# Attention with a routed mixture of experts: an own order for each of a batch's four attention periods, fixed PSUM places, and one FP32 product for a block of scores

## Chip, cores and metric

The kernel runs on one core of a Trainium2 chip. The metric is the device time of one execution in microseconds (us); of several executions the median is taken.

## What is computed

Eight batches, each with 8 heads of 576 positions by 64 dimensions, go through attention with a mask that lets a block of 64 positions see itself and the blocks before it. The result is 4608 rows of 512 numbers. Each row chooses one of 4 groups and in it one of 4 experts, is sent through that expert's two matrices (512 by 1024 and 1024 by 512, ReLU between) and is scaled by the two softmax weights.

```python
scores = scale * np.matmul(q, k.transpose(0, 1, 3, 2))
mask = block_i >= block_j                       # blocks of 64 positions
attn = softmax(np.where(mask, scores, -1e9))
x = np.matmul(attn, v).transpose(0, 2, 1, 3).reshape(4608, 512)
g_idx = argmax(x @ w_group);  e_idx = argmax(x @ w_expert[g_idx])
out[t] = g_w[t] * e_w[t] * (relu(x[t] @ w1[g, e]) @ w2[g, e])
```

## The kernel before

The program has an attention stage and an expert stage. Attention works on **head pairs**: pair `i` is two heads of one batch, 32 pairs in all, four to a batch. All five engines are scheduled by hand: each engine runs its instructions in the order in which the program writes them, and a semaphore holds an instruction back until its inputs are there and its output place is free.

**Periods and tokens.** `period` (line 357) is called with `x` from 0 on. It walks through a list of tokens, `ORDER` (lines 52 to 58); a token such as `S2@0` or `T1@1` is a step and a lag, and is done for pair `x - lag`. So one period mixes steps of several pairs, and one list serves all periods. A letter behind the lag says which engine drains a PSUM tile or does a conversion: `d` is DVE, `a` is ACT (POOL for `h` and `l`). The steps of a pair, with the line that does them:

- `K` (`prep`, line 160): the tiles of k and q are transposed by PE into PSUM; `k0`, `k1` (`full`) copy them to `nf`, as FP32. The last 64 positions of k and q go through another PSUM tile, the one that `V` fills (`flip_last`), and `j0`, `j1` (`full_last`) copy them to `nf`.
- `h0`, `h1` (`high`, line 191) round `nf` to FP32R (an FP32 number of fewer bits) in `qk`, k first and then q; `l0`, `l1` (`low`, line 196) subtract the rounded part, so that `qk` holds a high and a low part of each number. In the list `h0`, `h1` and `l1` are on POOL, `l0` on DVE.
- `S1`, `S2`, `S3`, `S8` (`score`, line 204): PE makes the scores as three products, high by high, high by low and low by high (`PROD`). `S2` also makes the scores of the first block of 128 queries, with the same three products into the columns from 384 of its PSUM tile. Two small products add the mask.
- `D` (`rowmax`, line 236) takes each row's maximum on DVE; `E0` to `E8` (`expo`, line 241) take the exponentials on ACT, with the row sums.
- `T1` to `T4` (`trans`, line 254): PE transposes the exponentials into PSUM; `t0` to `t4` (`drain`) copy them to `pt`. `V` (`values`, line 290) multiplies by v into the tile `o`; `v` copies that to `xT`.
- The **router's** steps `R`, `X`, `L`, `n`, `Y`, `M`, `G`, `Z` (`token`, line 649) exist once in a batch, not once in a pair: the logits, the choice of an expert, the writing of rows (`xd`) and of table entries (`tab`, `Z`). With one list for all, the lag alone decides in which of the four periods of a batch each of them falls.

The PSUM tiles of attention come from one pool of four places of two banks, handed out in turn (`wide`, line 94): the fifth tile that is asked for waits for the readers of the first.

The last period runs the list `END`. Its hooks (`timed`, in `attention_moe`) issue the first gathers and scatters of the expert stage. That stage is a list of groups of matmuls on PE, with the weights' loads and their splitting into high and low parts planned alongside; its last row store is split between ACT and DVE (`store`, lines 1160 and 1161). A loop for rows that did not fit (`overflow`, line 1341) follows; its count, `cnti`, is written by DVE in `spill`, and every engine loads it.

Of the kernel before, what the change touches and what calls it, by code (L numbers as in the profile page):

```python
# [8 lines left out]
F32 = mybir.dt.float32  # L9
# [5 lines left out]
ALU = mybir.AluOpType  # L15
# [52 lines left out]
class Attention:  # L68
    def __init__(self, tc, ctx, inner, q, k, v, consts):
# [9 lines left out]
        self.ps2 = self.psx.enter_context(tc.tile_pool(name="ps2", bufs=4, space=PSUM))  # L79
# [9 lines left out]
        self.mk = pfix.tile([P, 2, BLK], BF16, name="mk")  # L89
        self.lds, self.rs, self.xTs, self.sms = {}, {}, {}, {}  # L90
# [113 lines left out]
    def score(self, i, u):  # L204
# [17 lines left out]
        for u, c0 in ((2, 0), (0, 384)) if u == 2 else ((u, 0),):  # L222
            w = P * (u + 1)
            st = r["s", u] = ps[:, :, c0:c0 + w]
            for x, (hq, hk) in enumerate(self.PROD):
                for z in range(2):
                    p = slice(64 * z, 64 * z + 64)
                    nc.tensor.matmul(st[:, z, :], lhsT=t[p, hq, S + P * u:S + P * u + P], rhs=t[p, hk, 0:w],  # L228
                                     start=x == 0 and c0 == 0, stop=False)
        m = 2 if u == 0 else 1  # L230
# [93 lines left out]
    def start(self, N, order, on_dve, init):  # L324
# [17 lines left out]
        self.on_dve = on_dve  # L342
# [27 lines left out]
    def token(self, i, tok, N):  # L370
# [54 lines left out]
class Router:  # L425
# [187 lines left out]
    def spill(self, at, row, cnti):  # L613
# [32 lines left out]
        V.tensor_copy(cnti[0:1, 0:1], g[0:1, 0, R - 1:R])  # L646
        yield

    def token(self, at, b, tok):
# [61 lines left out]
        elif k == "Z":  # L711
            self.scatter(b, st, j, at.gate(at.now, 3) if j == 3 and not at.closed else None)
# [130 lines left out]
class Moe:  # L843
# [302 lines left out]
    def store(self, s, c, full):  # L1146
# [12 lines left out]
        elif s.get("o") == len(self.slots) - 1:  # L1159
            nc.scalar.activation(ys[0:n, 0:256], y[0:n, 0:256], AF.Copy, scale=cw[0:n])  # L1160
# [201 lines left out]
def attention_moe(ctx, tc, q, k, v, w_group, w_expert, w1, w2, out, order=None, on_dve=None):  # L1362
# [16 lines left out]
    with tc.manual_schedule(engines={ET.PE, ET.Activation, ET.DVE, ET.Pool, ET.SP}):  # L1379
# [81 lines left out]
        for _ in run:  # L1461
            pass
# [27 lines left out]
```

## Time and profile before

| what | value |
|---|---|
| median of 3 executions | 788.81 us (788.7 to 791.23) |
| the profiled execution | 785.75 us |
| its span, first to last instruction | 784.0 us |
| mean granted TensorE clock over the span | 0.996 |
| PE, ACT, DVE, POOL busy in the span | 97%, 64%, 69%, 45% |

The profile is of one execution. Engines are PE (matrix products; PEld is its weight load), ACT, DVE, POOL and SP (which issues most of the DMAs). Shares over the span average two stages: attention up to about 335 us, experts from there on. Each row of the page gives a source line, an engine, an operation, and output and input by the program's names.

### The profile page before, as it was taken

Reading aid. Unit: us, or ns where it says so; the run is one execution under the profiler, and the core shown is the slowest. Engines: PE = TensorE matmul, PEld = TensorE weight load, DVE = VectorE, ACT = ScalarE, POOL = GpSimd, SP = SyncE. Lnnn points to the kernel's source line nnn. Section 1 sums busy time; section 2 is a strip of 40 time slices with the busy share of each in tenths; the row PEclk is TensorE's granted clock in tenths of the full one; section 3 lists DMA queues with packets and bytes.
Section 4 is the critical chain, followed back from the end, with each engine's and each line's share of the span. In section 5 each row is a group of like instructions: output and inputs, shape, how many; then the busy total and the mean of one; then the engine's idle time right before and its main releaser. Section 6 shows DMA issues by size and latency. Waiting matters only on the chain.

```text
span 784.0 us, 20180 instructions
## 1 busy us (share of the span) xinstructions
PE 759.1 (97%) x7422; PEld 620.5 (79%) x7422; DVE 544.7 (69%) x1153; ACT 500.4 (64%) x1244; POOL 350.2 (45%) x481
## 2 busy tenths in 40 slices
PE   7899999999999999999999999999999999999996
PEld 4677777777777787768888788788988888888874
DVE  5567888888888888885454654754666667777742
ACT  5999999999999998755433433432434545545622
POOL 6444345454545454344143644454551553544212
PEclk9999999999999999999999999999999999999999
DMA  6478464646464636443779979979778897787771
GB/s 137 96 210 237 116 137 109 139 109 139 108 139 108 140 102 159 166 123 117 271 203 225 365 228 237 287 223 219 245 200 234 267 268 188 204 250 231 261 245 42
DMA packets 219108, 146.71 MB, mean 187 GB/s; under 512 B 155558, under 2 KB 186870, under 8 KB 219008
## 3 DMA queue, kind: packets, MB, share of 16 engines
q1 hardware_dynamic: 209920, 120.76, 57.6%
q0 software_dynamic: 9088, 24.64, 9.9%
q8 instruction: 60, 0.98, 0.5%
q14 instruction: 40, 0.33, 0.1%
HBM read 113.46 MB, written 24.59 MB: 176 GB/s over the span
## 4 chain that ended last, share of the span: by engine, by line
PE 80%; ACT 7%; DVE 6%; issue 3%; POOL 2%; DMA 2%; POOLq 0%; SPq 0%; ACTq 0%; DVEq 0%
PE h L1050 18%; PE y L1114 18%; PE o L313 10%; PE s L228 7%; PE tp L157 6%; PE h L1043 4%; PE s L218 3%; ACT pb L251 3%; PE ye L1114 3%; ACT pt L284 3%; PE he L1050 3%; PE y L1122 2%; DVE wl L949 1%; PE y L1133 1%; PE lg L690 1%
## 5 line engine op out<-in xcount | busy, mean ns | idle before, releaser
L1050 PE MATMUL h<-xt,wh 128*128 128x264 f32 (+6 forms) x704 | 156.3, 312 | 2.4 <-DVE xt L1010 2.3
L251 ACT ACTIVATE pb<-s,nm 128x128 f32<-128x128 f32 (+4 forms) x288 | 156.1, 568 | 3.5 <-DVE nm L239 1.6
L949 DVE TENSOR_TENSOR wl<-raw,wh 128x512 fp32r<-128x512 f32 x192 | 147.3, 804 | 8.5 <-ACT wh L948 8.4
L239 DVE TENSOR_REDUCE nm<-s 128x2 f32<-128x768 f32 (+4 forms) x160 | 126.3, 806 | 34.1 <-PE s L234 29.9
L1050 PEld LDWEIGHTS h<-xt,wh 128*128 128x128 f32 x704 | 119.2, 188 | 18.2 <-issue 4.2
L948 ACT CAST wh<-raw 128x512 fp32r<-128x512 f32 x192 | 109.6, 618 | 8.6 <-DMA raw<-in_moe_w_dram 6.0
L284 ACT COPY pt<-tp 128x1024 f32<-128x1024 f32 (+4 forms) x160 | 105.3, 696 | 8.6 <-PE tp L157 6.4
L1050 PE MATMUL h<-xt,wl 128*128 128x264 f32 (+6 forms) x352 | 109.2, 310 | 0.0
L1114 PE MATMUL y<-wh,hring 128*128 128x512 f32 x306 | 106.9, 400 | 0.4 <-ACT ys L1165 0.2
L228 PE MATMUL s<-qk 64*128 64x384 f32 (+3 forms) x768 | 89.9, 343 | 6.4 <-POOL qk L199 3.0
L1167 POOL DMA_INDIRECT out_dram<-ys,ids x40 | 47.0, 1174 | 108.1 <-DVE ys L1163 88.3
L313 PE MATMUL o<-pt,vb 128*64 128x320 f32 (+4 forms) x896 | 93.6, 360 | 0.4 <-DVE tmp L708 0.2
L194 POOL CAST qk<-nf 128x640 fp32r<-128x640 f32 (+1 forms) x63 | 42.7, 701 | 98.1 <-DVE nf L281 71.4
L313 PEld LDWEIGHTS o<-pt,vb 128*64 128x64 f32 x896 | 59.3, 137 | 32.2 <-DVE tmp L708 0.3
L157 PE MATMUL tp<-ident,pb 64*128 64x64 f32 x1600 | 76.3, 226 | 1.6 <-DVE xT L281 1.1
L228 PEld LDWEIGHTS s<-qk 64*128 64x128 f32 x768 | 61.6, 188 | 15.0 <-POOL qk L199 6.1
L157 PEld LDWEIGHTS tp<-ident,pb 64*128 64x128 f32 x1600 | 63.8, 140 | 10.2 <-ACT pb L251 3.9
L982 POOL COPY pl<-xg 128x1024 int16<-128x1024 int16 (+3 forms) x35 | 40.3, 1154 | 62.3 <-DMA xg<-xd,ids 40.6
L1114 PEld LDWEIGHTS y<-wh,hring 128*128 128x128 f32 x306 | 57.4, 188 | 13.1 <-DVE hring L1061 0.5
L1050 PEld LDWEIGHTS h<-xt,wl 128*128 128x128 f32 x352 | 66.2, 188 | 1.2
L251 ACT ACTIVATION_READ_ACCUMULATOR pb<-s,nm 128x1 f32 x288 | 64.1, 223 | 0.0
L199 POOL TENSOR_TENSOR qk<-nf,qk 128x640 fp32r<-128x640 f32 x31 | 61.2, 1975 | 2.6
(255 smaller groups left out, 1324.0 us busy)
## 6 DMA issues: line engine op xcount, KB each, us to landing
raw<-in_moe_w_dram SPq DMA_DIRECT2D x96, 512.0 KB, 4.2
rawq<-in_moe_w_dram SPq DMA_DIRECT2D x24, 512.0 KB, 7.8
natk<-in_k_dram SPq DMA_DIRECT2D x32, 256.0 KB, 3.6
natq<-in_q_dram SPq DMA_DIRECT2D x32, 256.0 KB, 5.5
vb<-in_v_dram SPq DMA_DIRECT2D x64, 128.0 KB, 2.8
wh<-in_moe_w_dram SPq DMA_DIRECT2D x16, 512.0 KB, 5.0
xd<-xns SPq DMA_DIRECT2D x12, 512.0 KB, 3.2
tab<-fill POOLq DMA_DIRECT2D x10, 512.0 KB, 4.1
```

The costliest lines, as they stand in the source:

```text
L157: self.nc.tensor.transpose(out=out[:, z], in_=src[r], identity=self.c["ident"][r, r])
L199: (eng or self.side(("l", n))).tensor_tensor(out=r["qk"][:, 1, o], in0=r["nf"][:, o], in1=r["qk"][:, 0, o].bitcast(F32), op=ALU.subtract)
L228: nc.tensor.matmul(st[:, z, :], lhsT=t[p, hq, S + P * u:S + P * u + P], rhs=t[p, hk, 0:w], start=x == 0 and c0 == 0, stop=False)
L239: self.nc.vector.tensor_reduce(out=o, in_=r["s", u], op=ALU.max, axis=ax, negate=True)
L251: nc.scalar.activation(reg, src, AF.Exp, bias=r["nm"][:, t:t + 1], accum_out=self.sms[b][:, pr, z, u:u + 1])
L284: return self.nc.scalar.copy(dst, src)
L313: nc.tensor.matmul(o[64 * a:64 * a + 64, hf, c0:c0 + BLK * (b1 - t)], lhsT=r["v"][:, a, j, :], rhs=pt[:, PTJ * j + t:PTJ * j + b1, a, :], ...
L948: nc.scalar.copy(h[:, sl], s["raw", u][:, sl])
L949: nc.vector.tensor_tensor(out=l[:, sl], in0=s["raw", u][:, sl], in1=h[:, sl].bitcast(F32), op=ALU.subtract)
L1050: nc.tensor.matmul(o, lhsT=ww[:, dc, f], rhs=rr[:, dc, t], start=dc == 0 and x == 0, stop=dc == 3 and x == 2)
L1114: nc.tensor.matmul(y[c][0:n], lhsT=hh, rhs=w, start=k == 0 and x == 0, stop=k == 7 and x == 2)
L1167: i = nc.gpsimd.indirect_dma_start(out=self.out, out_offset=bass.IndirectOffsetOnAxis(ap=s["ids"][0:n, c, 0:1], axis=0), in_=ys[0:n], in_o ...
```

## The change

1. `ORDER` becomes five lists. Period `x` runs list `x % 4`, and the first four periods run the fifth list. So each of a batch's four periods has its own order and its own choice of engines (`on_dve` is set anew in each period). `END` is another list as well.
2. The PSUM pool has one buffer for each of four tags, and a string of digits says for each tile, in the order in which tiles are asked for, which of the four places it takes.
3. `h` and `l` are cut differently: the first 512 columns of k and of q are rounded together in one instruction as soon as `k0` and `k1` are there, the last 64 of k and the last 128 of q apart from them (`kt`, `qt`); the low parts are four instructions, in three tokens.
4. The first block of scores, in `S2`, is one FP32 product of `nf` in place of the three FP32R products.
5. Every scatter `Z` is held back by the last row maximum written before it; `cnti` is copied by POOL, after the run; the last row store is ACT's alone; the hooks of the last periods sit at other places.

```diff
-ORDER, ON_DVE = parse("""
-Z2@7 E3@1 S2@0 D2@0 Z4@8 E2@1 n1@3a E8@1 T1@1 t3@1a t1@1a D0@0 K@-1 Z0@10 Y1@4 S3@0 D3@0 G2@6 R0@3
...
+ORDERS = [parse(t) for t in """
+t3@1a S2@0 E8@1 K@-1 S3@0 E2@1 V@2 E3@1 k1@-1a G0@5 k0@-1a D2@0 h0@-1a T2@1 D0@0 D3@0 S8@0 T1@1 Z4@9 E1@0 E4@0
+T4@1 E0@0 E5@0 E7@0 E6@0 G1@5 j1@-1d j0@-1d t0@1a v@2d h1@-1a l1@-1a l0@-1a S1@0 T3@0 l2@-1a D8@0 t2@1a t4@1d
+D1@0 t1@1a
+|
...
+""".split("|")]
...
+SLOTS = """
+3210123013201230213210312031231021302132130231023021031023103210231201302103231013202130231023021023021302310213
...
-        self.ps2 = self.psx.enter_context(tc.tile_pool(name="ps2", bufs=4, space=PSUM))
+        self.ps2 = self.psx.enter_context(tc.tile_pool(name="ps2", bufs=1, space=PSUM))
...
-        return self.ps2.tile([P, 2, 512], F32, tag="W", name=name)
+        return self.ps2.tile([P, 2, 512], F32, tag=f"W{next(self.slots)}", name=name)
...
+    def part(self, t, n):
+
+        if n == "kq":
+            return t[:, 0:2 * S].rearrange("p (n c) -> p n c", c=S)[:, :, 0:512]
+        return t[:, dict(k=slice(0, 512), q=slice(S, S + 512), kt=slice(512, S), qt=slice(S + 512, 2 * S + BLK))[n]]
...
-        (eng or self.side(("h", n))).tensor_copy(r["qk"][:, 0, o], r["nf"][:, o])
+        eng.tensor_copy(self.part(r["qk"][:, 0], n), self.part(r["nf"], n))
...
-        for u, c0 in ((2, 0), (0, 384)) if u == 2 else ((u, 0),):
-            w = P * (u + 1)
...
+        if m == 2:
+            st = r["s", 0] = ps[:, :, 384:512]
+            for z in range(2):
+                p = slice(64 * z, 64 * z + 64)
+                nc.tensor.matmul(st[:, z, :], lhsT=r["nf"][p, S:S + P], rhs=r["nf"][p, 0:P], start=True, stop=False)
...
+        self.last_gate = o[0:1, 0:1]
...
-        self.high(0, 0, nc.vector)
-        self.high(0, 1)
-        self.low(0, 0, nc.vector)
-        self.low(0, 1, nc.vector)
+        self.high(0, "k", nc.vector)
+        self.high(0, "q", nc.gpsimd)
+        self.low(0, "k", nc.vector)
+        self.low(0, "q", nc.vector)
+        for n in ("kt", "qt"):
+            self.high(0, n, nc.gpsimd)
+        for n in ("kt", "qt"):
+            self.low(0, n, nc.gpsimd)
...
-            self.high(i, tok[1])
+            for n in ("kt", "qt") if tok[1] else ("kq",):
+                self.high(i, n, self.side(tok))
         elif k == "l":
-            self.low(i, tok[1])
+            for n in (("k",), ("q",), ("kt", "qt"))[tok[1]]:
+                self.low(i, n, self.side(tok))
...
-        V.tensor_copy(cnti[0:1, 0:1], g[0:1, 0, R - 1:R])
+        self.over = g[0:1, 0, R - 1:R]
...
-            self.scatter(b, st, j, at.gate(at.now, 3) if j == 3 and not at.closed else None)
+            self.scatter(b, st, j, None if at.closed else at.last_gate)
...
-            nc.scalar.activation(ys[0:n, 0:256], y[0:n, 0:256], AF.Copy, scale=cw[0:n])
-            nc.vector.tensor_scalar(out=ys[0:n, 256:512], in0=y[0:n, 256:512], scalar1=cw[0:n], scalar2=None, op0=ALU.mult)
+            nc.scalar.activation(ys[0:n], y[0:n], AF.Copy, scale=cw[0:n])
...
+            order, at.on_dve = ORDERS[x % 4 if x > 3 else 4]
...
             for _ in run:
             pass
+        nc.gpsimd.tensor_copy(cnti, ro.over)
```

What the new lists do to the engines is seen in the instructions that each engine gets. In a row, `L` is the line, then the operation, and the tile it writes and those it reads. The first place is POOL in one steady period (the third batch's, one pair). Before:

```order
L812 MEMSET mark 1x1
L819 DMA tab<-pay_163,pi_2026 82560x16
L779 IOTA pay_164 128x5
L194 CAST qk_113<-nf_115 128x576
L194 CAST qk_113<-nf_115 128x640
L199 TENSOR_TENSOR qk_113<-nf_115,qk_113 128x640
```

and with the change:

```order
L851 COPY mark<-nm_2470 1x1
L856 DMA tab<-pay_163,pi_2032 82560x16
L221 CAST qk_114<-nf_116 128x64
L221 CAST qk_114<-nf_116 128x128
L225 TENSOR_TENSOR qk_114<-nf_116,qk_114 128x512 x2
L225 TENSOR_TENSOR qk_114<-nf_116,qk_114 128x64
L225 TENSOR_TENSOR qk_114<-nf_116,qk_114 128x128
L221 CAST qk_113<-nf_115 128x2x512
```

Both low parts of the 512 columns are now POOL's, the rounding of the next pair (`128x2x512`) stands ahead of everything that needs the last columns, and the scatter's hold copies from `nm`, the row maxima, where a MEMSET stood.

The second place is PE at the step `S2`, in the same batch. Before:

```order
L157 MATMUL tp_3_2470<-ident,pb_120 128x64 x16
L228 MATMUL s_2_2499<-qk_113 128x384 x6
L228 MATMUL s_2_2499<-qk_113 128x128 x6
L234 LDWEIGHTS mq
L234 MATMUL s_2_2499<-mk,mq 128x2x64
```

and with the change:

```order
L253 MATMUL s_2_2471<-nf_115 128x128 x2
L259 MATMUL s_2_2471<-qk_113 128x384 x6
L265 LDWEIGHTS mq
L265 MATMUL s_2_2471<-mk,mq 128x2x64
```

Two products of `nf` stand ahead of the six of `qk`, in place of six behind them.

The third place is ACT over most of one period. Before:

```order
L251 ACTIVATE pb_119,sm_2496<-s_3_2546,nm_2498 128x512 x2
L284 COPY pt_2469<-tp_2_2581 128x2x3x128
L738 ACTIVATE eex_2629<-edd_2625 128x20
L284 COPY pt_2469<-tp_2_2581 128x256
L284 COPY pt_2469<-tp_4_2609 128x2x5x64
L251 ACTIVATE pb_119,sm_2496<-s_1_2598,nm_2498 128x256 x2
L251 ACTIVATE pb_119,sm_2496<-s_8_2636,nm_2498 128x576
L284 COPY pt_2676<-tp_3_2677 128x2x4x128
L284 COPY pt_2676<-tp_1_2722 128x2x2x128
L284 COPY nf_115<-tp_2734 128x512
L285 ACTIVATE nf_115<-tp_2734 128x512
```

and with the change, in the period whose list has both logit copies (`lt`):

```order
L316 COPY lt<-lg_1_2850 128x2x288
L316 COPY lt<-lg_0_2859 128x2x288
L316 COPY pt_2893<-tp_3_2894 128x2x4x128
L283 ACTIVATE pb_120,sm_2468<-s_1_2881,nm_2685 128x256 x2
L283 ACTIVATE pb_119,sm_2468<-s_3_2921,nm_2920 128x512 x2
L316 COPY nf_116<-tp_2947 128x512
L283 ACTIVATE pb_119,sm_2468<-s_2_2932,nm_2920 128x384 x2
L283 ACTIVATE pb_119,sm_2468<-s_2_2932,nm_2920 128x128 x2
L316 COPY pt_2893<-tp_1_2998 128x2x2x128
L316 COPY pt_2893<-tp_2_3010 128x256
L316 COPY pt_2893<-tp_2_3010 128x2x3x128
```

One of the two copies to `nf` and the copy of `tp_4` are gone from ACT in this period. Over the whole program ACT has 13 scaled and 10 plain copies to `nf` fewer, 7, 3 and 17 copies to `pt` fewer (of 256, 768 and 640 columns), and 11 copies to `xT` (576 columns) more; DVE has the reverse, and 23 subtractions fewer. On PE, between two `V` steps of a steady batch, 15 instructions wait for PE itself before, and 7 with the change.

## Rows read from the trace of the kernel before

**Rows 1.** Page, part 1: busy time, share of the span, instructions

```profile
PE 759.1 (97%) x7422; PEld 620.5 (79%) x7422; DVE 544.7 (69%) x1153; ACT 500.4 (64%) x1244; POOL 350.2 (45%) x481
```

**Rows 2.** Windows by stage: start:end length, busy (instructions), granted PE clock, DMA share, GB/s

```profile
19.20:28.80 9.60, 7.87 (x113) 6.66 (x111) 5.85 (x9) 9.37 (x27) 4.33 (x5) 0.82 0.48 96
...
106.74:117.08 10.34, 10.20 (x172) 7.92 (x171) 8.60 (x16) 10.05 (x28) 4.75 (x7) 1.00 0.78 173
...
126.44:135.76 9.32, 9.32 (x152) 7.49 (x153) 8.03 (x17) 9.18 (x27) 4.49 (x6) 1.00 0.61 150
...
185.18:224.43 39.25, 38.84 (x629) 30.59 (x631) 33.83 (x77) 37.62 (x105) 19.20 (x26) 1.00 0.52 124
...
303.52:321.13 17.61, 15.89 (x237) 12.00 (x238) 14.13 (x34) 14.19 (x42) 8.71 (x13) 1.00 0.72 215
```

**Rows 3.** The chain of waits in attention, several windows: start us, length us, what

```profile
53.69 1.94 POOL qk L199
...
58.02 2.85 PE o L313 x28
...
102.15 0.73 PE lg L690 x16
...
114.62 1.40 ACT pt L284 x2
...
130.01 0.45 PE s L228 x6
...
131.86 0.65 PE xn L157 x16
...
133.00 1.13 PE s L228 x12
...
134.96 0.76 PE s L228 x6
```

**Rows 4.** Timeline: start us, us, engine, line, operation, count [idle before <-releaser]

```profile
36.55 0.58 PEld L228 LDWEIGHTS s<-qk 64*128 64x128 f32 x8 [1.32 <-POOL qk L199]
...
55.67 0.58 PEld L228 LDWEIGHTS s<-qk 64*128 64x128 f32 x8 [1.21 <-POOL qk L199]
...
101.02 1.03 PE L218 MATMUL s<-qk 128*128 128x288 f32 x6
101.89 0.21 PE L789 MATMUL rk<-o,tri 128*128 128x80 bf16 x1
...
130.83 1.02 PE L218 MATMUL s<-qk 128*128 128x288 f32 x6
131.79 0.72 PE L157 MATMUL xn<-ident,xT 64*128 64x64 f32 x16
...
133.41 0.58 PEld L228 LDWEIGHTS s<-qk 64*128 64x128 f32 x8 [0.21 <-POOL qk L199]
```

**Rows 5.** Groups by line and form, 0 to 335 us: busy, mean ns, idle before

```profile
L199 POOL TENSOR_TENSOR qk<-nf,qk 128x640 fp32r<-128x640 f32 x31 | 61.2, 1975 | 2.6
L199 DVE TENSOR_TENSOR qk<-nf,qk 128x576 fp32r<-128x576 f32 x32 | 26.6, 830 | 0.3
L281 DVE COPY xT<-o 128x576 f32<-128x576 f32 x32 | 23.9, 748 | 0.1
L194 POOL CAST qk<-nf 128x640 fp32r<-128x640 f32 x32 | 23.6, 737 | 1.9 <-DVE nf L282 1.9
L284 ACT COPY pt<-tp 128x640 f32<-128x640 f32 x32 | 22.7, 708 | 0.5 <-PE tp L157 0.5
L284 ACT COPY nf<-tp 128x512 f32<-128x512 f32 x32 | 18.9, 591 | 10.5 <-PE tp L157 10.5
```

**Rows 6.** Timeline of the program's end

```profile
776.97 0.47 ACT L1160 ACTIVATE ys<-y,ids 128x256 f32<-128x256 f32 x1 [4.94 <-PE y L1114]
778.02 0.48 DVE L1161 TENSOR_SCALAR ys<-y,ids 128x256 f32<-128x256 f32 x1 [5.27 <-ACTq L1342]
778.79 0.99 POOL L1167 DMA_INDIRECT out_dram<-ys,ids  x1 [5.81 <-DVE ys L1161]
```

More of the change, by code (lines that the diff above doesn't have):

```diff
@@ new lines @@
+E6@0 Z0@10 E7@0 j0@-1d E1@0 E0@0 h1@-1a v@2d l1@-1a t2@1a S8@0 T1@1 t0@1d l0@-1a t4@1a D8@0 X1@6 L1@2 L0@2 G4@6
+t1@1a G3@6 S1@0 D1@0 l2@-1a T3@0
+|
+E8@1 S3@0 D3@0 n1@3a S2@0 n0@3a D0@0 t3@1a E2@1 K@-1 D2@0 E3@1 E6@0 V@2 Z2@7 R0@3 E7@0 T1@1 k0@-1a E5@0 E4@0
+T2@1 E0@0 k1@-1d v@2d E1@0 T4@1 j0@-1d t1@1a h0@-1a T3@0 t0@1a S1@0 l0@-1a j1@-1d t4@1d D1@0 l1@-1a X2@3 h1@-1a
+l2@-1a S8@0 t2@1a D8@0
+|
+S2@0 t3@1a D0@0 S3@0 E2@1 K@-1 D2@0 E3@1 E8@1 D3@0 k0@-1d k1@-1d Z3@8 V@2 h0@-1a T4@1 l0@-1a E0@0 Y1@4 E4@0
@@ new lines @@
+j0@-1d Y0@4 T2@1 j1@-1d E1@0 E7@0 M1@4 E5@0 E6@0 t4@1a T3@0 l1@-1a T1@1 h1@-1a M0@4 S8@0 v@2a l2@-1a t2@1a D8@0
+t1@1a Z1@8 S1@0 t0@1a D1@0
+|
+K@-1 S3@0 E8@1 t3@1a k0@-1d E2@1 S2@0 V@2 k1@-1a D3@0 D2@0 T2@1 h0@-1a l0@-1a S8@0 E3@1 D0@0 E7@0 T1@1 E6@0 E4@0
+E5@0 E0@0 T4@1 j0@-1d j1@-1d t2@1d E1@0 v@2a t0@1a D8@0 h1@-1a t4@1d l1@-1a T3@0 t1@1a l2@-1d S1@0 D1@0
+""".split("|")]
+END, END_DVE = parse("""
+t3@2a Y1@5 E2@2 E3@2 E8@2 S2@1 T1@2 Y0@5 M1@5 D2@1 t1@2a T4@2 M0@5 S3@1 T2@2 t4@2a E4@1 E5@1 t2@2a V@3 S1@1 D0@1
@@ L65 @@
+1320321032013210231201302103123210213021023012301230123012
+"""
 LAST = [("G", 0), ("G", 1), ("G", 2), ("G", 4), ("G", 3)] + [("X", j) for j in range(3)]
@@ L189, in side, with high, low @@
         return self.nc.vector if tok in self.on_dve else self.nc.gpsimd
-    def high(self, i, n, eng=None):
+    def part(self, t, n):
+        if n == "kq":
+            return t[:, 0:2 * S].rearrange("p (n c) -> p n c", c=S)[:, :, 0:512]
+        return t[:, dict(k=slice(0, 512), q=slice(S, S + 512), kt=slice(512, S), qt=slice(S + 512, 2 * S + BLK))[n]]
+    def high(self, i, n, eng):
         r = self.rs[i]
-        o = slice(S, 2 * S + BLK) if n else slice(0, S)
-        (eng or self.side(("h", n))).tensor_copy(r["qk"][:, 0, o], r["nf"][:, o])
-    def low(self, i, n, eng=None):
+        eng.tensor_copy(self.part(r["qk"][:, 0], n), self.part(r["nf"], n))
+    def low(self, i, n, eng):
         r = self.rs[i]
-        o = slice(S, 2 * S + BLK) if n else slice(0, S)
-        (eng or self.side(("l", n))).tensor_tensor(out=r["qk"][:, 1, o], in0=r["nf"][:, o], in1=r["qk"][:, 0, o].bitcast(F32),
-                                              op=ALU.subtract)
+        eng.tensor_tensor(out=self.part(r["qk"][:, 1], n), in0=self.part(r["nf"], n),
+                          in1=self.part(r["qk"][:, 0], n).bitcast(F32), op=ALU.subtract)
     PROD = ((0, 0), (0, 1), (1, 0))
@@ L221, in score @@
             return
-        for u, c0 in ((2, 0), (0, 384)) if u == 2 else ((u, 0),):
-            w = P * (u + 1)
[L224 to L230, printed above, removed]
+        m = 2 if u == 2 else 1
+        if m == 2:
[3 more added lines that the diff above has]
+                nc.tensor.matmul(st[:, z, :], lhsT=r["nf"][p, S:S + P], rhs=r["nf"][p, 0:P], start=True, stop=False)
+        c0, w = 0, P * (u + 1)
+        st = r["s", u] = ps[:, :, 0:w]
+        for x, (hq, hk) in enumerate(self.PROD):
+            for z in range(2):
+                p = slice(64 * z, 64 * z + 64)
+                nc.tensor.matmul(st[:, z, :], lhsT=t[p, hq, S + P * u:S + P * u + P], rhs=t[p, hk, 0:w],
+                                 start=x == 0 and m == 1, stop=False)
+        w += P * (m - 1)
         for z in range(2):
@@ L611, in final, with spill @@
         yield
-    def spill(self, at, row, cnti):
+    def spill(self, at, row):
         nc = self.nc
@@ L1361, in attention_moe @@
 @with_exitstack
-def attention_moe(ctx, tc, q, k, v, w_group, w_expert, w1, w2, out, order=None, on_dve=None):
+def attention_moe(ctx, tc, q, k, v, w_group, w_expert, w1, w2, out):
     nc = tc.nc
-    order = order or ORDER
-    on_dve = ON_DVE if on_dve is None else on_dve
     NBAT = q.shape[0]
@@ L1387, in attention_moe @@
         at.masks()
[L1388 removed]
+        at.start(N, ro.constants)
         pre, fil = ro.setup(), ro.table()
@@ L1434, in attention_moe @@
         }
-        spl = ro.spill(at, rowo, cnti)
+        spl = ro.spill(at, rowo)
         for n in (60, 63, 65, 67, 68, 69):
```

27 lines of the change are left out of this document (13 added, 14 removed).

## The prediction

> **What bounds the kernel now.** I read the page's busy shares first, then one batch of attention in the windows by stage, then the chain of waits, to see which engine the time of a batch really runs along. PE is busy 97% of the span [rows 1], but a busy PE is not a PE at its peak, and DVE and ACT at 69% and 64% are averages over two stages. The window of one steady batch tells more [rows 2]: of 39.25 us ACT is busy for 37.62, PE for 38.84, DVE for 33.83, POOL for 19.20. Two engines are full at once. The granted clock there is 1.00, so nothing is lost to the clock.
>
> Which of the two sets the pace differs from period to period. The period from 126.44 to 135.76 takes 9.32 us, and its chain runs along PE without a break. The one from 106.74 to 117.08 takes 10.34 with ACT busy for 10.05 of it [rows 2], and its chain goes over to ACT (1.40 us of `pt` copies at 114.62 are one piece [rows 3]). A batch has two periods of each kind.
>
> What PE itself needs for a batch follows from the quick period: 9.32, less the router's transposes `xn` (0.65) [rows 3] and less a wait of 0.21 for POOL's low part [rows 4], is 8.46 us for one pair. Four pairs are 33.8. The router adds two groups of logits at 0.73 and two of `xn` at 0.65 [rows 3], a half one of `xn`, and the logits' transposes and ranks, which I put at 1.2 by their number of matmuls: 4.0. So PE needs 37.8, and 1.4 of the 39.25 is ACT's.
>
> Inside those 37.8 there are waits of PE for itself. The step `S8` takes 0.96 where the next instruction waits for PE (130.83 to 131.79) and 0.87 where it doesn't (101.02 to 101.89) [rows 4]: 0.09 us each.
>
> **The change part by part: steady batches.**
>
> *ACT's relief.* ACT loses 23 copies to `nf` at 0.591, 17 copies of 640 columns at 0.708 [rows 5], and ten others, put at 0.5; it gains 11 copies of 576 columns, put at 0.65. That is 13.6 + 12.0 + 5 - 7.2 = 23.4 us over 32 pairs, 2.9 a batch: 34.7 in place of 37.6. DVE takes these over: 23 at about 0.67 and 17 at about 0.8 (from 0.748 for 576 columns), ten at 0.5, less 11 at 0.748 and less 23 subtractions at 0.83 [rows 5]: 6.5 us in all, 0.8 a batch, 34.6 in place of 33.8. ACT therefore stops being the bound if a batch takes 37 to 38, and DVE stands at 92%. What hides the added DVE work is the idle time that it has now, 5.4 us a batch; if that is in the wrong places, row maxima come late and the exponentials behind them.
>
> *PE's waits for itself.* 15 a batch become 7: 8 x 0.09 = 0.7 us. Below, this is 0, where PE waits for something else at the same place.
>
> *The first block in FP32.* The trace of before has no FP32 score, so I bound it. The twelve products of `S2` take 1.13 with a wait of 0.21 in it; six of 256 columns take 0.45 and six of 512 take 0.76, so six of 384 take 0.605 [rows 3, 4], and the first block's six take 0.31. The nearest FP32 products are those of `o`: 2.85 us for 1600 columns in a half, 1.78 ns each [rows 3], so 0.23 for 128 columns. I take the gain of 0.08 a pair, 0.3 a batch; the ends are 0.31 (it hides altogether) and -0.15 (the two heads' products run one behind the other, 0.46). By the Trainium skill's page "FP8 and Floating Point Precision" (TensorE Precision Notes) true FP32 makes four passes; against three of one pass each, that would lose one pass of 128 columns at 2.4 GHz, 0.05 us a pair, an estimate by which the sum would be some 4 us smaller. No row prices it for this shape, but those of `o` speak for the smaller price.
>
> *POOL's part.* Per pair POOL had two roundings and a subtraction of 1.975. Now it has a rounding of 1024 columns (1.1, from 0.737 for 640), two subtractions of 512 columns (1.58 each, in proportion) [rows 5], and small pieces, put at 1.1 together: 5.4 in place of 3.4, 27 a batch of 37.6. It has room; the question is when the parts come. The rounding no longer stands behind the last 64 positions, which PE transposes only after `V`, so it starts earlier; the two subtractions now run one behind the other, 3.2 us, where DVE (0.83) and POOL (1.98) ran side by side. Queued behind them are small pieces and the next scatter, whose hold now waits for a row maximum; the scatter's table is read only in the expert stage, but what stands behind the hold waits with it. I leave PE 0.2 us of waiting a period, as today [rows 4], 0.8 a batch. The fixed PSUM places add no instruction; what they take away is counted in the waits.
>
> A batch then takes 37.8 - 0.7 - 0.3 + 0.8 = 37.6 us, 1.65 less. From the `V` at 58.02 [rows 3] to 303.52 there are 245.5 us, 6.25 batches: **10.3 us**.
>
> **The rest.** In the periods without a router, up to 58 us, PE waits for POOL's low part once in each: 1.32 at 36.55 and 1.21 at 55.67 are the first and the last of three [rows 4], and the chain goes through POOL (1.94 at 53.69) [rows 3]. POOL begins there only behind the last positions; begun earlier, 1.1 of each wait goes: **3.3** (ends 0 and 3.6). Before that, from 19.20 to 28.80, ACT is busy for 9.37 of 9.60 at a granted clock of 0.82, a mean between the two levels [rows 2]; the fifth list takes one `nf` copy and three `pt` copies from it. I take **1.2** (0 to 3). From 303.52 to 321.13 PE is busy for 15.89 of 17.61 [rows 2], so 1.7 is there for `END`; I take **0.7**, between -1 and 1.7. At the end, DVE's half of the last store starts 0.58 after ACT's, held by the loop's instructions, and POOL's scatter starts at 778.79 [rows 6]. With ACT alone, whose 512 columns I put at 0.7, and the same 0.29 to the issue, it starts at 777.96: **0.8**. The `cnti` copy and the loads behind it lie beside the scatter's landing. The expert stage keeps its instructions and moves forward whole; I cost it at nothing, which holds as long as its weights come in time.
>
> The sum is 10.3 + 3.3 + 1.2 + 0.7 + 0.8 = 16.3 us. The profiled execution took 785.75 (span 784.0 and 1.75 around it), which becomes 769.4; the median of the runs shown lies 3.06 higher, at 788.81, and becomes **772.5**.
>
> **The rivals.**
> - *Slower: POOL's chain takes the place of ACT's copies.* The rounding and two subtractions are 4.3 us from `k1` to the last score part. Where PE has less than that to do in between, it waits, as it waited 1.32 and 1.21 in the fill [rows 4]. For it: POOL pays 3.1 ns a column, DVE 1.44 [rows 5]. Against it: all lists but one put the rounding before `V` or close behind it, whose 2.85 and the transposes after it cover the 4.3. Over 28 periods it decides from 16.3 / 28 = 0.58 us a period on; at 1.2 a period it gives -16.3 + 34 = 17 us more, 806; I put it at 800. The Trainium skill's "GPSIMD Engine Reference" (4.1, Engine selection) speaks for this rival: it would keep two-input work on VectorE, as about twice as slow on GPSIMD. The rows here show 2.1 times, so the trace agrees on the price; whether it lies on the path is open. 7%.
> - *Little gain.* DVE at 92% hands the row maxima on late, or steps between the engines are too tight, and a batch stays at 39: only the fill, the end and part of the waits are left, 4 to 6 us, 784. For it: 92% busy with many small router steps. Against it: today ACT runs at 96%. 18%.
> - *More.* PE waits for nothing: 36.8 a batch and a clock that doesn't drop in the fill, 7 us more, 765. 8%.
> - *Nothing left over:* gains and new waits cancel, 788. 2%.
>
> **How the numbers follow.** The forecast has 65%. Range: from 765 (the full relief) to 786 (little gain and its bound), which leaves out the slower rival, the cancelling one and parts of two others, some 17%. What a measurement of this kernel can tell from no change is about 0.3%, 2.4 us. Faster: 65 + 8 + 14 of the 18 = 87%; within 0.3%: the other 4 and 2 = 6%; slower 7%.
>
> **What would show it.** In the profile after: a batch of 37.6 us with PE at over 98% and ACT near 34.7; no wait of over 0.5 us for `qk` below 58 us; the scatter of the last store directly behind ACT's copy; the two FP32 products at 0.23 us. I am wrong if the waits of PE name POOL's subtractions in steady periods, if DVE's row maxima release ACT, or if the expert stage grows by what attention gave.

## The result and the profile after

The changed kernel takes **781.79 us** (median of 4 executions, 780.46 to 784.61), the kernel before 788.75 beside it: ratio 0.9917, 95% interval 0.9895 to 0.9938. That is 7.0 us less, where 16.3 were forecast (772.5). The profiled execution of the changed kernel is the longest of its four, 784.61 (span 782.5).

Page, part 1, of the changed kernel, to set beside [rows 1]:

```profile
PE 754.8 (96%) x7358; PEld 615.4 (79%) x7358; DVE 550.8 (70%) x1167; ACT 482.6 (62%) x1205; POOL 394.4 (50%) x602
```

For the parts of the time I use marks that both traces have: the first `V` of a pair, the fourth, the twenty-ninth, the experts' first product, the end of the last `y` matmul. They bound the start, the fill, the steady part, END, the expert stage and, to the end of the span, the tail. Windows between the first four marks, in the kernel before (columns as in [rows 2]):

```profile
28.69:57.95 29.26, 26.69 (x403) 20.83 (x400) 17.17 (x27) 27.35 (x76) 14.44 (x18) 1.00 0.66 165
57.95:303.45 245.50, 242.59 (x3915) 190.71 (x3912) 210.28 (x481) 235.29 (x651) 116.66 (x156) 1.00 0.55 132
303.45:331.45 28.00, 26.21 (x387) 19.94 (x383) 22.95 (x55) 22.74 (x59) 12.86 (x21) 1.00 0.62 189
```

and in the changed kernel, with one steady batch and its four periods behind them:

```profile
27.58:54.16 26.58, 26.38 (x396) 20.56 (x394) 19.21 (x34) 24.72 (x73) 17.31 (x26) 1.00 0.62 165
54.16:295.22 241.06, 239.03 (x3882) 185.65 (x3878) 211.88 (x488) 221.18 (x619) 152.36 (x255) 1.00 0.54 136
295.22:323.16 27.94, 26.21 (x378) 19.94 (x374) 22.09 (x56) 22.70 (x58) 15.26 (x27) 1.00 0.62 189
178.75:217.01 38.26, 38.16 (x623) 29.70 (x620) 33.89 (x79) 35.28 (x99) 25.05 (x42) 1.00 0.52 125
178.75:187.74 8.99, 8.99 (x144) 7.01 (x140) 7.90 (x19) 7.97 (x23) 6.15 (x11) 1.00 0.43 96
187.74:197.05 9.31, 9.31 (x156) 7.47 (x153) 8.19 (x18) 8.78 (x24) 7.21 (x12) 1.00 0.79 176
197.05:206.49 9.44, 9.35 (x153) 7.35 (x149) 8.91 (x19) 9.31 (x28) 5.75 (x9) 1.00 0.51 118
206.49:217.01 10.52, 10.51 (x186) 7.88 (x183) 8.89 (x27) 9.22 (x25) 5.95 (x10) 1.00 0.37 112
```

The start is 1.1 us shorter, the fill 2.7, the steady part only 4.4, END 0.1: attention gives 8.3. In this batch ACT fell to 35.28 (34.7 forecast) and POOL rose to 25.05 (27), and ACT no longer fills any period but the third; yet the batch takes 38.26, not 37.6. From the `V` of a pair to that of the next, mean of the steady part, by the pair's place in its batch (b_fp32 is an experiment below):

| kernel | first | second | third | fourth |
|---|---|---|---|---|
| before | 10.47 | 9.33 | 9.32 | 10.11 |
| b_fp32 | 10.47 | 9.11 | 9.11 | 10.10 |
| changed | 9.33 | 9.30 | 9.39 | 10.42 |

The gain is all in the first period. The fourth, which has both groups of logits now, grew, and the two quick ones stayed as they were.

The program's end in the changed kernel, beside [rows 6]:

```profile
772.41 0.39 PE L1151 MATMUL y<-wh,hring 128*128 128x512 f32 x1
772.84 0.69 ACT L1197 ACTIVATE ys<-y,ids 128x512 f32<-128x512 f32 x1 [4.94 <-PE y L1151]
773.80 0.99 POOL L1203 DMA_INDIRECT out_dram<-ys,ids  x1 [4.97 <-ACT ys L1197]
774.77 0.18 POOL L1501 CAST cnti<-fin 1x1 int32<-1x1 f32 x1
```

The scatter starts 1.0 us behind the last matmul, where it was 1.86 before (776.93 to 778.79). But from there to the end of the span it is 8.74 us, before 5.23: the end, from the last matmul on, grew from 7.1 to 9.7. The expert stage (first product to last matmul) took 445.5 before and 449.6 after in these two executions; more on that below.

By kind of step, from the first start of a step to that of the next, summed over the 25 pairs of the steady part: the first block's scores -3.3 us, the logits -1.7, `S3` -1.6, the logits' transposes of `Y` (tile `ly`) -1.1, `S2` -0.9, `S1` -0.3; `K` +1.9, **`S8` +1.2**, the rest +1.3.

### The profile page after: what moved, and what is told of

It is laid out like the page before. It is cut to its first block, busy times and chain, and to the rows that moved or that the text cites. A ratio compares the mean times of both kernels' runs of the same rounds, so it can differ in the third digit from the quotient of the medians.

```text
span 782.5 us, 20027 instructions
## 1 busy us (share of the span) xinstructions
PE 754.8 (96%) x7358; PEld 615.4 (79%) x7358; DVE 550.8 (70%) x1167; ACT 482.6 (62%) x1205; POOL 394.4 (50%) x602
## 4 chain that ended last, share of the span: by engine, by line
PE 79%; DVE 5%; ACT 4%; issue 4%; DMA 3%; POOL 3%; SPq 1%; POOLq 0%; DVEq 0%; ACTq 0%
PE h L1087 17%; PE y L1151 17%; PE o L345 10%; PE tp L179 9%; PE s L259 7%; PE h L1080 4%; PE s L244 3%; ACT pb L283 2%; PE y L1159 2%; PE he L1087 2%; PE ye L1151 1%; DVE wl L986 1%; PE y L1170 1%; PE lg L727 1%; PE s L253 1%
## 5 line engine op out<-in xcount | busy, mean ns | idle before, releaser
L283 ACT ACTIVATE pb<-s,nm 128x256 f32<-128x256 f32 (+4 forms) x288 | 156.1, 559 | 12.1 <-DVE nm L270 9.2
L270 DVE TENSOR_REDUCE nm<-s 128x2 f32<-128x1024 f32 (+4 forms) x160 | 123.1, 805 | 12.4 <-PE s L265 9.0
L225 POOL TENSOR_TENSOR qk<-nf,qk 128x512 fp32r<-128x512 f32 (+1 forms) x118 | 98.2, 853 | 1.4
L316 ACT COPY pt<-tp 128x1024 f32<-128x1024 f32 (+4 forms) x133 | 88.9, 724 | 16.0 <-PE tp L179 12.9
L221 POOL CAST qk<-nf 128x128 fp32r<-128x128 f32 (+3 forms) x96 | 48.9, 529 | 55.2 <-ACT nf L317 19.7
L259 PE MATMUL s<-qk 64*128 64x512 f32 (+2 forms) x576 | 75.0, 366 | 1.5 <-POOL qk L225 1.0
L179 PE MATMUL tp<-ident,pb 64*128 64x64 f32 x1600 | 68.9, 228 | 3.9 <-ACT pb L283 1.5
L179 PEld LDWEIGHTS tp<-ident,pb 64*128 64x128 f32 x1600 | 59.5, 140 | 9.1 <-ACT pb L283 2.2
L283 ACT ACTIVATION_READ_ACCUMULATOR pb<-s,nm 128x1 f32 x288 | 60.8, 211 | 0.0
L1151 PE MATMUL y<-wl,hring 128*128 128x512 f32 x153 | 60.6, 396 | 0.0
```

The costliest lines, as they stand in the source:

```text
L179: self.nc.tensor.transpose(out=out[:, z], in_=src[r], identity=self.c["ident"][r, r])
L221: eng.tensor_copy(self.part(r["qk"][:, 0], n), self.part(r["nf"], n))
L225: eng.tensor_tensor(out=self.part(r["qk"][:, 1], n), in0=self.part(r["nf"], n), in1=self.part(r["qk"][:, 0], n).bitcast(F32), op=ALU.subtract)
L283: nc.scalar.activation(reg, src, AF.Exp, bias=r["nm"][:, t:t + 1], accum_out=self.sms[b][:, pr, z, u:u + 1])
L316: return self.nc.scalar.copy(dst, src)
L1151: nc.tensor.matmul(y[c][0:n], lhsT=hh, rhs=w, start=k == 0 and x == 0, stop=k == 7 and x == 2)
```

## Experiments

All times in us; each kernel's marks are from its own profile, its ratio is to the kernel before on the same chip. In the four kernels with the same attention (changed, a_same, a_cnti, a_cnti_split) the steady part repeats to 0.4 and the tail, where it is the same, to 0.1; a_rr and a_best, also alike in attention, differ by 0.8 in the steady part.

| kernel | median | ratio (95%) | fill | steady | END | experts | tail |
|---|---|---|---|---|---|---|---|
| before | 788.75 | 1 | 29.26 | 245.50 | 28.00 | 445.5 | 7.09 |
| changed | 781.79 | 0.9917 (0.9895-0.9938) | 26.58 | 241.06 | 27.94 | 449.6 | 9.74 |
| a_same | 782.34 | 0.9909 (0.9879-0.9938) | 26.58 | 240.96 | 27.83 | 452.3 | 9.77 |
| a_cnti | 779.22 | 0.9879 (0.9851-0.9907) | 26.59 | 240.66 | 27.77 | 447.7 | 7.01 |
| a_cnti_split | 780.20 | 0.9896 (0.9863-0.9929) | 26.58 | 240.65 | 28.04 | 444.8 | 7.10 |
| a_fp32r | 784.26 | 0.9950 (0.9923-0.9976) | 27.28 | 243.73 | 27.71 | 446.1 | 9.75 |
| b_fp32 | 782.95 | 0.9945 (0.9924-0.9966) | 28.52 | 242.84 | 27.86 | 445.9 | 7.09 |
| b_cut | 785.70 | 0.9982 (0.9962-1.0002) | 29.25 | 243.67 | 27.65 | 445.4 | 7.09 |
| a_cut | 778.38 | 0.9896 (0.9857-0.9935) | 26.42 | 237.55 | 26.40 | 446.8 | 10.26 |
| a_actback | 810.04 | 1.0285 (1.0246-1.0323) | 26.89 | 269.36 | 27.95 | 446.0 | 9.82 |
| a_rr | 780.48 | 0.9924 (0.9894-0.9953) | 26.78 | 241.41 | 26.63 | 446.4 | 9.82 |
| a_oldlist | 798.70 | 1.0155 (1.0121-1.0189) | 27.90 | 254.36 | 27.84 | 448.2 | 9.81 |
| b_relief | 805.16 | 1.0237 (1.0152-1.0323) | 29.26 | 261.19 | 28.43 | 450.2 | 7.10 |
| a_t4back | 785.76 | 0.9984 (0.9967-1.0001) | 26.91 | 246.63 | 26.78 | 446.6 | 9.82 |
| a_rk | 784.59 | 0.9926 (0.9903-0.9950) | 26.77 | 244.09 | 27.95 | 446.8 | 9.74 |
| a_best | 778.49 | 0.9855 (0.9834-0.9876) | 26.77 | 242.22 | 27.92 | 444.9 | 7.02 |

### The tail and the expert stage

**a_same**, no edit. 

> The changed kernel, once more as it is, so that the other runs have it beside them on the same chip. About 781.8 us, 7 less than the kernel before. In its first profile the expert stage (first product of the experts to the last matmul) took 449.7 us where the kernel before took 445.5, with two long waits for DMAs in it. If these waits belong to the change they come again at the same places; if they vary from execution to execution they are gone or elsewhere, and the stage takes 445 to 447.

The stage took 452.3. PE's longest waits there, first in the profile of the changed kernel, then in this one (columns: who waited for whom, us in total, times, longest):

```profile
PE h L1080 <- DMA wh<-in_moe_w_dram: 2.2, 1, 2.2
```

```profile
PE h L1080 <- DMA wh<-in_moe_w_dram: 3.8, 2, 3.0
```

So the wait for weights came again, between 480 and 530 us. Over all kernels it was between 0.2 and 3.8 in 11 of 16 profiles, and absent in the kernel before and in four more, two of them versions of the changed kernel (a_cnti_split, a_fp32r). It varies between executions; it came in 10 of the 12 profiles of a changed kernel and in one of the four of the kernel before and its versions. Whether the change makes it more frequent stays open. In the two profiles shown here the granted clock from 480 to 530 us is 0.97 in the mean, and 1.00 in the kernel before: another 1.5 us, an estimate from these numbers. With the wait of 2.2 this is most of the 4.1 by which the stage of the changed kernel's profile is longer.

**a_cnti.**

```diff
-        self.over = g[0:1, 0, R - 1:R]
+        V.tensor_copy(cnti[0:1, 0:1], g[0:1, 0, R - 1:R])
...
-        nc.gpsimd.tensor_copy(cnti, ro.over)
```

> The changed kernel with one part undone: the loop's count is copied by DVE inside the expert stage, as before, and not by POOL behind the last scatter; the last row store stays ACT's alone. Theory one: the stretch from the last y matmul to the end grew from 7.1 to 9.7 us because the loads of the count, and the loop's instructions, now begin behind the last scatter; then this version is 2.5 to 3.4 us faster than the changed kernel and the stretch takes 6.3 to 7.2. Rival: the stretch is set by the landing of the last scatter, which the copy doesn't touch; then it is within 0.5 us of the changed kernel.

**a_cnti_split**: the same, and the last store in two halves. 

> The whole tail undone: the count by DVE inside the stage, and the last store split between ACT and DVE, as before. If the store by ACT alone was worth the 0.8 us that I had forecast, this is 0.8 slower than the version with the count alone moved back; if DVE's half is held only by the loop's instructions, which then lie elsewhere, the two are within 0.3.

The tail went to 7.01 and 7.10: theory one, and no gain from the store by ACT alone. The end of a_cnti:

```profile
769.41 0.39 PE L1151 MATMUL y<-wh,hring 128*128 128x512 f32 x1
769.84 0.69 ACT L1197 ACTIVATE ys<-y,ids 128x512 f32<-128x512 f32 x1 [4.94 <-PE y L1151]
771.57 0.99 POOL L1203 DMA_INDIRECT out_dram<-ys,ids  x1 [5.72 <-ACTq L1378]
```

With the count early, POOL's scatter is issued behind the loop's instructions, 1.0 us after ACT's copy is done, but nothing is left to do behind it: 5.24 to the end of the span. The changed kernel issues the scatter 0.8 earlier and then goes through the loads of the count and the loop, 8.74: by its trace all engines load the count at 775.0, and POOL, the last, is through the loop's instructions at 778.3, 3.5 us behind the end of the scatter's issue.

### What the first block in FP32 is worth

**a_fp32r**: in the changed kernel the two FP32 products are six FP32R products again.

```diff
-                nc.tensor.matmul(st[:, z, :], lhsT=r["nf"][p, S:S + P], rhs=r["nf"][p, 0:P], start=True, stop=False)
+                for x, (hq, hk) in enumerate(self.PROD):
+                    nc.tensor.matmul(st[:, z, :], lhsT=t[p, hq, S:S + P], rhs=t[p, hk, 0:P],
+                                     start=x == 0, stop=False)
```

> The changed kernel with the first block's scores as three FP32R products again, in place of one FP32 product. Theory one: steady batches run along PE, so what PE saves per pair (0.08 us) counts: 32 x 0.08 = 2.6 us slower than the changed kernel. Rival: the gain is swallowed by waits for other engines, 0 to 1 us slower; or the FP32 products were no gain and this is faster.

**b_fp32**: the same replacement, the other way, alone in the kernel before. 

> The kernel before with one part of the change alone: the first block's scores as one FP32 product. Undoing it in the changed kernel lengthened the steady batches (from the second V that I marked, at 58 us, to the one at 303) by 2.8 us of 25 pairs, and the fill by 0.7. Theory A, PE sets the pace of the kernel before as well, ACT's 37.6 of 39.25 is only a share: the same gain here, 2.3 to 3.3 in the steady batches. Theory B, the one of the prediction, ACT sets the pace in two of the four periods: what PE saves there is lost, 1.4 or less.

The steady part: +2.7 in the one, -2.7 in the other. So this one edit is worth 60% of the steady gain (4.4) in either kernel. That is theory A's number, but theory A, that PE alone sets the pace, falls with the next two runs.

### What PE's time is worth

**b_cut, a_cut**: two of `S8`'s six products left out in either kernel.

```diff
-                for x, (hq, hk) in enumerate(self.PROD):
+                for x, (hq, hk) in enumerate(self.PROD[:2]):
```

> The kernel before without the third product (low by high) of the step S8: of its six matmuls of 288 columns two are left out, some 0.29 us of PE's work per pair, and nothing of another engine's. Over the 25 steady pairs this is 7.2 us. Theory A (PE alone sets the pace): 6 to 7.2 us less. Theory B (ACT is a second bound, at 37.6 of 39.25 in the mean and full in two of four periods): a batch can't lose 1.15, the steady part loses 2 to 4.

> The changed kernel with the same cut: the third product (low by high) of the step S8 is left out. ACT is busy for 35.3 of 38.2 there. Theory A: 6 to 7.2 us less in the steady part. Theory B says the same here, since ACT has room for 1.15 a batch; so the two kernels' difference tells. A third theory C, that waits between the engines (a step hands on late, wherever PE's work is) fill what PE saves: under 4 in both.

The `S8` steps of the 25 pairs took 6.5 us less in both. The steady part took 1.8 less in the kernel before and 3.5 in the changed one: under 4 in both, theory C. The quick periods of the kernel before, which I had read as PE's own, stayed at 9.32. Where the saving went is a wait at the start of `S2`, here before (ACT and PEld, from the `V` at 156.22)

```profile
162.42 0.23 ACT L251 ACTIVATION_READ_ACCUMULATOR pb<-s,nm 128x1 f32 x1
162.71 0.33 PEld L228 LDWEIGHTS s<-qk 64*128 64x128 f32 x4
163.26 0.30 PEld L228 LDWEIGHTS s<-qk 64*128 64x128 f32 x4 [0.22 <-POOL qk L199]
```

and in b_cut (from the `V` at 156.81), with POOL's subtraction:

```profile
163.00 0.23 ACT L251 ACTIVATION_READ_ACCUMULATOR pb<-s,nm 128x1 f32 x1
163.30 0.33 PEld L228 LDWEIGHTS s<-qk 64*128 64x128 f32 x4 [0.25 <-issue]
163.85 0.30 PEld L228 LDWEIGHTS s<-qk 64*128 64x128 f32 x4 [0.22 <-POOL qk L199]
...
161.81 1.98 POOL L199 TENSOR_TENSOR qk<-nf,qk 128x640 fp32r<-128x640 f32 x1
```

`S2` starts 6.5 us behind the `V` in all twelve quick periods of both, and in b_cut the weight loads have stood idle for 0.25 by then. The line names no releaser, but by its semaphores PE waits there for DVE and ACT, and ACT's signal, at the end of an exponential (6.42 behind the `V`), is the last. In the kernel before PE reached `S2` just then, and so the chain named PE alone. POOL's low part ends 7.0 us behind the `V` in both (161.22 + 1.99 before, 161.81 + 1.98 here), and the second half of `S2` waits the same 0.22 for it. In b_fp32 the products of `nf`, which need no low part, stand in that second gap, and the quick periods fall to 9.1. In the longer of the two slow periods (10.38 before, 10.29 in b_cut, 10.39 in b_fp32) neither edit did much: there ACT is busy for 10.1, though no run tests that by itself. In the other slow period (10.11 before, 9.97 in b_cut) about half of the 0.26 counted. So PE's time alone set the pace of no period of the kernel before: the quick ones were held at ACT's exponential and at POOL's low part.

### What ACT's relief is worth

**a_actback**, the drains' letters as before: `t4@1d` to `t4@1a` twice, `t0@1d` to `t0@1a`, `k1@-1d` and `k0@-1d` to `a`, `v@2a` to `v@2d` in the fourth list. 

> The changed kernel with the drains given back in periods 0 to 3: the copies t4 and t0 and the copies k0 and k1, which the lists had moved to DVE, are ACT's again, and the xT copy v of one period is DVE's. ACT's work returns to about 37.5 us a batch, DVE's falls to about 32. Theory B: the relief of ACT gave the steady gain, so it goes: 4 us or more slower in the steady part. Theory A: the relief gave little, 0 to 2 us slower.

**a_t4back**, the first three letters alone. 

> The changed kernel with three drains a batch given back to ACT, t4 in periods 0 and 2 and t0 in period 1, and nothing else (the copies to nf and the one to xT stay with their new engines; in the run before this the xT copy on DVE held PE's transposes up by some 2 us in each fourth period). ACT rises from 35.3 to about 37.1 of 38.5 us. Theory B: 4 us or more slower in the steady part. Rival: 0 to 2 slower.

**b_relief**, in the kernel before:

```diff
+            if x:
+                at.on_dve = on_dve | {(("t", 4), ("t", 0), ("t", 4), ("t", 4))[x % 4]}
+                if x % 4 == 3:
+                    at.on_dve = on_dve
```

> The kernel before with ACT's relief alone: in periods 0 and 2 of each batch the copy t4, in period 1 the copy t0, goes to DVE, at the same place of the list (period 3 as it was). ACT falls from 37.6 to about 35.9 us a batch, DVE rises from 33.8 to about 35.8. Theory B of the prediction (1.4 of each batch's 39.25 is ACT's): 3 to 9 us less in the steady part. The rival after the cuts (every PE step waits a little for what the step before last handed out, and the time saved at one place is waited for at the next): between 2 less and 3 more.

a_actback lost 28.3, more than either theory allows: the `xT` copy, at its place in the list but on DVE, held PE's transposes up by 1.9 at a time, and 20.6 of the 28.3 fall in that one period of the batch, so the run says little on ACT's copies. a_t4back is the clean one: 5.6 slower, 0.89 a batch, and its chain goes over to ACT from 181.68 to 187.5:

```profile
180.42 1.24 DVE nm L270
...
183.60 1.84 ACT pb L283 x8
185.44 2.06 ACT pt L316 x4
```

Theory B holds there: 4.6 of the 5.6 fall in the third period (9.39 to 10.16), the one that ACT fills in the changed kernel. Yet b_relief, the same relief in the old list, is 15.7 slower (two executions). Its chain in one period:

```profile
159.24 0.76 DVE nm L239
160.00 0.74 DVE pt L281
160.74 0.14 issue
160.88 1.08 PE s L228 x12
```

The moved copy stands behind the row maximum of `S8` in DVE's order, and `S2` waits for the place that it frees. So the relief has its worth in the new order and none in the old one.

### Lists and places

**a_oldlist**: one list, `END`, scatters, hooks and the pool of before, with `l2` behind `l1`; the rest as changed. 

> The changed kernel with its five lists and END taken out: all periods run the one list of before (with the low part of the last columns behind that of q), the scatters and the last hooks sit where they sat, the places come from the pool; FP32 product, the new cut of the roundings and the new tail stay. FP32 alone in the kernel before gave a steady part of 242.8 us, against 245.5 before and 241.0 in the changed kernel. If the lists gave what is left: 242 to 244. Rival: the new cut of POOL's parts needs the new lists, and POOL's subtractions come late in the old one: 250 or more.

**a_rr**: only the places back to the pool.

```diff
-        self.ps2 = self.psx.enter_context(tc.tile_pool(name="ps2", bufs=1, space=PSUM))
+        self.ps2 = self.psx.enter_context(tc.tile_pool(name="ps2", bufs=4, space=PSUM))
...
-        return self.ps2.tile([P, 2, 512], F32, tag=f"W{next(self.slots)}", name=name)
+        return self.ps2.tile([P, 2, 512], F32, tag="W", name=name)
```

> The changed kernel with the PSUM places handed out by the pool, as before, and not by the string of digits; every engine's order stays as it is. Theory A of the steady part (PE's own steps plus a small wait at nearly every change of step): 0 to 1.5 us slower, in the steps that start a new tile (K, S512, tp). Rival: the fixed places are what lets the new lists run; then a tile waits for a late reader in each period, and the steady part is 4 us slower or more.

The fixed places are worth 0.4 here (1.6 by a_best against a_cnti, below; the two versions without them differ by 0.8). With the old list the rest of the change loses: 254.4, 8.9 more than before. That is the rival's number, but not its cause: POOL stands nowhere on the chain of the steady part. PE's longest wait is for the `xT` copy (8.0 us, 11 times), and ahead of that copy in DVE's order is a small instruction that took 1.76 us five times, beside POOL's scatter and the new rounding of 1024 columns:

```profile
159.14 1.76 DVE L757 SCALAR_TENSOR_TENSOR gsc<-gdd,desc 128x20 f32<-128x20 f32 x1
158.81 1.00 POOL L837 DMA_INDIRECT tab<-pay,pi  x1 [0.51 <-issue]
159.81 1.05 POOL L202 CAST qk<-nf 128x1024 fp32r<-128x1024 f32 x1
```

In the kernel before and in the changed one it takes 0.18. The five periods with it took 10.6, the same period of the first steady batch, without it, 9.3: 6.5 of the 8.9. Which of POOL's two instructions holds it, no run separates.

### The step S8

**a_rk**: in the second list `G4@6` stands behind `S8@0`, places from the pool. 

> The changed kernel with the places from the pool, and the step G4 (the three rank products, whose bf16 weights are loaded by an instruction of their own) moved to stand directly behind S8 in the period of list 1, in each batch once. Its first load waits for DVE and its first product for PE. From S8's last product to the next start it is 0.22 us now, whoever is waited for. Theory of the prediction (a wait of PE for itself costs 0.09): it stays at 0.22 with rk behind S8, since rk waits too. Rival (the form of what follows sets it): 0.13, as in the kernel before where rk followed S8, in six places of the steady part, and 0.22 elsewhere. The time as a whole moves by less than 1 us either way.

PE around `S8` in a_rr, and in a_rk:

```profile
172.11 1.05 PE L244 MATMUL s<-qk 128*128 128x288 f32 x6
173.10 0.46 PE L179 MATMUL tp<-ident,pb 64*128 64x64 f32 x8
```

```profile
173.66 1.06 PE L244 MATMUL s<-qk 128*128 128x288 f32 x6
174.56 0.21 PE L826 MATMUL rk<-o,tri 128*128 128x80 bf16 x1
```

From `S8`'s last product to the next start it is 0.220 us in a_rr and 0.130 in a_rk, in all six places, though `rk` waits for DVE and for PE. The rival holds: what follows sets it, and not a wait. The kernel as a whole became 2.7 slower in the steady part, which I had not expected: `rk` no longer stands between the logits and `S1`, and `xn` and the logits, now earlier, waited 0.25 each; each such period took 10.88 in place of 10.52.

### The best version

**a_best**: a_cnti and a_rr together. 

> The changed kernel with its count copied by DVE inside the expert stage, as before, and its PSUM places from the pool. The first gave a tail of 7.0 us in place of 9.7, the second 0.4 more in the steady part and 1.2 less in END. If these add up: attention ends (first product of the experts) 0.6 to 1.0 us sooner than in the changed kernel, the tail is 7.0 to 7.2, and the median is 3.3 to 3.7 us below the changed kernel's, about 778.7. Rival: the END gain was chance, and it equals the version with the count alone, 779.2.

The tail's gain is there (7.02), END's is not: END is 26.4 to 26.8 in three kernels and 27.7 to 28.4 in all others, this one included; it varies, and its cause is open. The median is 778.49, against 779.22 for a_cnti: the two can't be told apart. The ratio of a_best lies below that of the changed kernel beyond both intervals; that of a_cnti overlaps it, and what the count by DVE is worth is read from the tail.

## Why the prediction was wrong

- **The steady batches, 10.3 forecast, 4.4 measured.** The step that failed is *PE's waits for itself*: 0.7 us a batch, 8 x 0.09, for 15 such waits that become 7. I had compared an `S8` step of 0.96, with a wait for PE behind it, with one of 0.87, "where it doesn't" wait [rows 4]. It is the other way round. The instruction behind the short one does wait for PE, as PE's order in the kernel before shows:

```
L218 MATMUL s_8_1996<-qk_114 128x288 x5
L789 LDWEIGHTS tri [waits PE_49]
```

  and by the trace's semaphores what stands behind the 19 long ones of the steady part waits for ACT alone. In the changed kernel seven of the 25 `S8` steps have a wait for PE behind them and 18 have none, and it is 0.22 to the next start in all. So these waits cost nothing that the traces show; what shortens the step is `rk`, whose product begins 0.09 sooner than an FP32 one in its place. Its weights are bf16, and an instruction of its own loads them; which of the two it is, no run separates. The Trainium skill's page "TensorE: Matmul & The Clock Gate" (Weight-path perf modes) says that weights of full width go in faster if they are not FP32; these traces agree, with 0.10 us for a load of `rk` and 0.19 for one of `S8`. The changed kernel puts no `rk` behind `S8` any more, which is 0.54 of the 1.16 us by which these steps grew; the other 0.62 lies between the first two products of the step, and its cause is open. Together this is 0.19 a batch more, in place of 0.7 less.

  Three more terms were off. The router's terms add up to 4.3 and not 4.0, so PE's need was 38.1 by my own rows, and the steady batches 8.5 and not 10.3. The FP32 product gave 0.43 a batch, not 0.3. PE's wait for POOL's low part, left at 0.8 a batch, was 0.5 us in all. With these four as measured a batch would be 1.3 shorter; 0.71 was measured. What is missing shows in the quick periods, 9.30 and 9.39 where b_fp32 has 9.11; ACT fills the second of them, and for the first the cause is open.
- **ACT's relief.** The size of the move was right (34.7 forecast, 35.28 measured, DVE 34.6 and 33.89), and undoing three of its copies cost 0.89 a batch. But "PE needs 37.8" was not PE's need: time taken from PE in a quick period was waited for at ACT's exponential, and POOL's low part came behind that. My sign that DVE's row maxima release ACT did come, before and after:

```profile
L251 ACT ACTIVATE pb<-s,nm 128x128 f32<-128x128 f32 (+4 forms) x288 | 156.1, 568 | 3.5 <-DVE nm L239 1.6
L283 ACT ACTIVATE pb<-s,nm 128x256 f32<-128x256 f32 (+4 forms) x288 | 156.1, 559 | 12.1 <-DVE nm L270 9.2
```

  On the chain of the steady part row maxima are 3.7 us, 2.0 before, so this is at most a small part of the miss.
- **FP32 price.** 0.23 forecast, 0.22 measured (5.54 us over 25 pairs). The Trainium skill's page "FP8 and Floating Point Precision" (TensorE Precision Notes) gives true FP32 four passes; by an estimate from that, 0.21 for 128 columns at 2.4 GHz, the price agrees with the trace. By the same estimate the FP32R products that it replaces, three passes, would take 0.16; the trace doesn't agree, with 0.35. My rows had put those six at 0.31, and they took 0.35 (8.85 us over 25 pairs): that was the mis-sized part. The FP32 product also needs no low part, so its saving was not waited for at POOL.
- **POOL.** Its part was right (27 forecast, 25.05), its rival did not come. PE's waits for POOL's low part from the first `V` to about the twenty-ninth, before and after (weight loads, columns as above), and POOL's prices after:

```profile
PEld s L228 <- POOL qk L199: 5.3, 12, 1.3
```

```profile
PEld s L259 <- POOL qk L225: 0.5, 1, 0.5
```

```profile
L225 POOL TENSOR_TENSOR qk<-nf,qk 128x512 fp32r<-128x512 f32 x62 | 78.2, 1276 | 1.4
L221 POOL CAST qk<-nf 128x1024 fp32r<-128x1024 f32 x31 | 32.2, 1038 | 38.3 <-ACT nf L317 19.7 <-ACT nf L316 14.0 <-DVE nf L314 4.6
```

  I had put 1.58 and 1.1: the 1.975 that I scaled from held a delay by DVE's own subtraction (last section).
- **Fill and start**: 3.3 and 1.2 forecast, 2.7 and 1.1 measured. PE is now busy for 26.38 of 26.58 there. Right in the main, but 0.7 of the 2.7 is the FP32 product's (a_fp32r), which I had not counted there.
- **END**: 0.7 forecast, 0.1 measured, within what it varies.
- **The tail**: 0.8 less forecast, 2.65 more measured. The scatter did start 0.86 earlier against the last matmul (DVE's half had started 0.58 behind the end of ACT's, 1.05 behind its start). What failed is the sentence that the `cnti` copy and the loads behind it lie beside the scatter's landing and so cost nothing: they begin only behind its issue and lengthen the end, as a_cnti shows. I saw the copy move and did not follow who waits for it: every engine.
- **The expert stage**, put at nothing: 444.8 to 452.3 in all profiles, with the same instructions; the change has no part in it that these runs can show. The medians (7.0 less) fit attention and tail (8.3 - 2.65 = 5.7) within their interval of some 1.7.

## What to carry to other kernels

Before a short and a long instance of a step are put down to a wait, look at what follows each and whether it waits too; a difference can lie in the form of the next instruction. A saving is worth its size only up to the next wait with a fixed end, so list the waits behind it, here ACT's exponential and POOL's low part; an edit that needs no such input keeps its gain. What is moved to the very end of a program has everyone who reads it behind it.

## What was not expected of the hardware

- From the start of `S8`'s last product to the next start it is 0.219 to 0.225 us where an FP32 or FP32R product or a transpose follows, and 0.130 to 0.135 where `rk` does, with its bf16 weights, whether or not the follower waits for PE.
- POOL's subtraction of 512 columns takes 1.276 us, that of 640 took 1.975 in the kernel before [rows 5]: 2.5 and 3.1 ns a column. The traces show why. In 29 of the 31 cases DVE's subtraction had begun before POOL's, and POOL's took 1.92 to 2.12; in the two others it took 1.54, 2.4 ns a column. In b_relief it took 1.54 to 1.57 nine times; in seven of them DVE's subtraction began behind POOL's and took 1.01 to 1.47 in place of 0.75. Where the two run side by side, the one that begins later takes longer.
